# A decode layer on one core: the last weight matrix in two halves, its tail rows in one DMA, zero products between waits

## The chip, the cores and the metric

The kernel runs on one core of one Trainium2 chip. The metric is device time in microseconds (us), the median of several executions; the other cores are idle.

Names: PE is the matrix engine (TensorE), PEld its weight loads, DVE VectorE, ACT ScalarE, POOL GpSimd, SP SyncE, which issues most DMAs. SPq and ACTq are the DMA queues of SP and ACT.

## The reference, cut to what matters

```python
# A: attention over a cache, one query row per batch; B: a dense layer with mish
x = A_x                                           # (4, 1, 640)
h = x + A_ref(layernorm(x), k_cache, v_cache, wq, wo)   # caches (4, 32, 4096, 128) bf16
def B_ref(x, w1, b1, w2):                         # w1 (640, 1728), w2 (1728, 640)
    h = x @ w1 + b1
    act = h * tanh(softplus(h))
    return act @ w2
h2 = h + B_ref(layernorm(h), w1, b1, w2)
```

All arrays are bf16. The caches are 2 x 134 MB, nearly all of the traffic. The change concerns the short end: after the attention come wo, w1 and w2, 10 MB of weights, and the output of 4 x 640 numbers.

## The kernel before: the parts that matter

1728 = 13 x 128 + 64. So w2 has 13 full blocks of 128 rows (`FM` = 13) and a tail of 64 rows (`FT`). The full blocks are loaded in pieces: with runs of n rows, partition p holds n neighbouring rows of w2 in one contiguous packet of n x 1280 bytes (the trace has them: 5120 bytes for a run of 4 rows).

```python
    # SP: weights queue behind each other: wo, w1, the w2 tail, then w2 in 4 pieces
    w1_v = B_w1.rearrange("(p c) n -> p c n", c=DC)
    for k, (c0, c1) in enumerate(zip(W1S, W1S[1:])):          # three pieces
        load(sp, w1_sb[:, c0:c1, :], w1_v[:, c0:c1, :], ("w1", c0), f"W{len(WOS) + k}")
    for k in range(FT // 8):                                  # eight DMAs of 8 rows
        r = slice(k // 4 * 32 + k % 4, k // 4 * 32 + 32, 4)   # partitions 4 apart
        load(sp, w2_tail[r, :], B_w2[FM * P : F, :][r, :], ("w2t", k), "WT")
    ...
    for k, (j0, j1) in enumerate(zip(W2S, W2S[1:])):          # 4, 4, 4, 1 rows
        load(sp, w2_sb[:, j0:j1, :],
             B_w2[j0 * P : j1 * P, :].rearrange("(p j) n -> p j n", j=j1 - j0), ("w2", j0), ...)

    # PE: zero products whose result nobody reads; they keep PE busy
    def busy(n):
        for _ in range(n):
            mm(o_full[:, :], ident[:, :], zeros[:, 0:1].to_broadcast([P, 512]), True, True)
    ...
    busy(4)
    pe.need("act")
    def w2_mm(j):                     # one w2 row: four products of 160 columns
        rows = P if j < FM else FT    # on four column groups of PE, side by side
        for k in range(CG):
            cs = slice(k * OC, (k + 1) * OC)
            done = j == FM - 1 and k == CG - 1
            mm(y2_ps[k * QD : k * QD + N, :], act[0:rows, j, :],
               w2_sb[:, j, cs] if j < FM else w2_tail[0:FT, cs], False, j == FM - 1,
               "y2" if done else None)
    pe.need(("w2t", FT // 8 - 1))
    w2_mm(FM)
    for j0, j1 in zip(W2S, W2S[1:]):
        pe.need(("w2", j0))           # wait for this piece
        for j in range(j0, j1):
            w2_mm(j)

    # DVE casts all four quarters at once; SP and ACT issue two stores each
    dv.need("y2")
    dv.do(lambda: v.tensor_copy(out=o_bf[:, :], in_=y2_ps), "o_bf", DV)
```

Each list is the program of one engine, in its order; `need` is a wait on a semaphore. The engines work side by side in the timeline (at 653.03 us ACT, DVE and PE each start an operation), and so do the four products of a w2 row: a row takes 0.069 us at full clock though it streams 640 columns in all, where a zero product of 512 columns takes 0.22 us.

The softmax here doesn't subtract the row's maximum and nothing guards it: scores larger than these inputs give would overflow.

## Time and profile before

| | before |
|---|---|
| time, median of the first 3 runs | 661.67 us |
| span of the profiled run | 660.0 us |
| DMA engines busy | 90% or more in all slices but the last |
| act (input of w2's products) ready | 654.54 us |
| last two w2 pieces landed | 657.19 and 657.57 us |
| last product, last cast ended | 657.86, 658.23 us |

From the page of before, its first part and two lines on DMA. In the second line each digit is the busy share of a fortieth of the span in tenths, 9 meaning 90% or more.

```profile
span 660.0 us, 4989 instructions
...
PE 383.8 (58%) x2636; PEld 68.4 (10%) x1680; DVE 407.8 (62%) x257; ACT 40.7 (6%) x157; POOL 1.7 (0%) x12
...
DMA  9999999999999999999999999999999999999997
...
DMA packets 6954, 283.50 MB, mean 430 GB/s; under 512 B 857, under 2 KB 1184, under 8 KB 2208
```

The DMA engines are full until the last slice: the kernel is bound by moving 283.5 MB at 430 GB/s. The end is read from the timeline: start in us, length in us, engine, line, operation, number of instructions, and what ended the idle time before it.

```profile
653.49 1.49 PE L730 MATMUL o_ps<-zeros,ident 128*128 128x512 bf16 x3 [0.21 <-DMA w_tail<-in_B_w_dram]
...
655.13 1.27 PE L730 MATMUL red<-slotA,act 128*4 128x160 bf16 x32
...
657.23 0.62 PE L730 MATMUL red<-slotA,act 128*4 128x160 bf16 x20 [0.83 <-DMA slotA<-in_B_w_dram]
657.91 0.32 DVE L726 CAST o_bf<-red 128x160 bf16<-128x160 f32 x1 [3.37 <-PE red L730]
658.26 0.65 SPq L263 DMA_DIRECT2D out_dram<-o_bf  x2
```

PE runs through eight w2 rows, then waits for the last two pieces, and needs 0.62 us for their five rows; then come a cast and two stores on each queue. A wait of a group is printed only where it is long, and some records of products are missing: of the four zero products the first line has three. The windows view (length, then busy time and number of instructions of each engine, then the granted share of PE's clock, DMA share and GB/s) shows that PE ran at half its clock from about 653.4 to 656.8, without harm, since it waited for DMA afterwards:

```profile
650.00:652.00 2.00, 1.34 (x38) 1.21 (x35) 0.00 (x0) 0.47 (x1) 0.00 (x0) 1.00 1.05 407
652.00:654.00 2.00, 1.79 (x60) 1.43 (x59) 1.03 (x5) 0.25 (x1) 0.00 (x0) 0.84 1.00 410
654.00:656.00 2.00, 2.00 (x35) 0.81 (x37) 0.51 (x2) 0.00 (x0) 0.00 (x0) 0.50 0.86 345
```

The trace also has every DMA packet with its size and duration, and the time of each completion. A load of 128 rows leaves 16 of these reports; the eight 8-row DMAs of the tail left 72 (eight before 641.8 us, and 64 from 650.27 to 653.26). The trace does not name the DMA engine of a packet or of a report. "First", "mean" and "last" landing below are over the reports of one load.

### The profile page before, as it was taken

The page shows a single profiled execution, that of the slowest core. Times are in us where ns is not written, and L with a number is a line of the kernel's source. Part 1 is how long each engine was busy: PE and PEld are TensorE (multiplying, and loading weights), DVE is VectorE, ACT ScalarE, POOL GpSimd, SP SyncE. Part 2 cuts the span into 40 slices and gives each one's busy share as a digit, 9 for nine tenths or more (in the row PEclk, how much of TensorE's full clock was granted, in tenths as well). Part 3 has the DMA queues.
Part 4 walks back from the last instruction along what each step waited for, and adds up shares of the span by engine and source line. Part 5 has one row for each costly group of instructions (what it writes and reads, how often), then busy time and mean ns, then how long its engine had stood idle before and what let it go on. Part 6 is the DMA issues. An engine that isn't in the chain of part 4 may idle for free. (4 is left out here: it accounts for less than half of the span.)

```text
span 660.0 us, 4989 instructions
## 1 busy us (share of the span) xinstructions
PE 383.8 (58%) x2636; PEld 68.4 (10%) x1680; DVE 407.8 (62%) x257; ACT 40.7 (6%) x157; POOL 1.7 (0%) x12
## 2 busy tenths in 40 slices
PE   1255758457327595838307395838434757665877
PEld 0000100101101010101100010000110001010145
DVE  1087988386048778677219798749206688957612
ACT  0200000000000000000000000000000000000011
POOL 0000000000000000000000000000000000000000
PEclk9778787879659796869668887879876769796868
DMA  9999999999999999999999999999999999999997
GB/s 418 409 445 445 438 441 417 422 441 438 438 437 425 429 437 437 441 437 421 433 437 437 441 437 417 437 437 433 441 441 417 437 433 437 441 441 417 425 416 312
DMA packets 6954, 283.50 MB, mean 430 GB/s; under 512 B 857, under 2 KB 1184, under 8 KB 2208
## 3 DMA queue, kind: packets, MB, share of 16 engines
q1 hardware_dynamic: 6912, 283.35, 99.4%
q8 instruction: 7, 0.11, 0.1%
q14 instruction: 3, 0.02, 0.0%
q10 hardware_dynamic: 32, 0.01, 0.0%
HBM read 283.35 MB, written 0.01 MB: 429 GB/s over the span
## 5 line engine op out<-in xcount | busy, mean ns | idle before, releaser
L529 DVE TENSOR_TENSOR slotA<-slotA,q_bc 128x8192 bf16<-128x8192 bf16 x32 | 140.7, 4416 | 93.1 <-DMA slotA<-in_A_k_cache_dram 93.1
L529 DVE TENSOR_TENSOR slotB<-slotB,q_bc 128x8192 bf16<-128x8192 bf16 x32 | 140.7, 4418 | 18.4 <-DMA slotB<-in_A_k_cache_dram 18.4
L540 DVE TENSOR_REDUCE s_f<-red 128x64 f32<-128x1024 f32 x64 | 78.0, 1219 | 96.3 <-PE red L740 96.2
L740 PE MATMUL red<-slotA,ident 128*128 128x512 bf16 x480 | 135.8, 446 | 0.0
L740 PE MATMUL red<-slotB,ident 128*128 128x512 bf16 x480 | 126.1, 422 | 0.0
L730 PE MATMUL red<-slotA,ident 128*128 128x512 bf16 x32 | 14.7, 458 | 129.4 <-PEq L49 129.4
L730 PE MATMUL pv<-slotC,e 128*32 128x512 bf16 x768 | 51.9, 430 | 37.3 <-PEq L49 34.3
L730 PE MATMUL red<-slotB,ident 128*128 128x512 bf16 x32 | 14.2, 443 | 89.1 <-PEq L49 89.1
L406 ACT ACTIVATE ex<-s_f 128x64 bf16<-128x64 f32 x64 | 16.4, 256 | 513.3 <-DVE s_f L540 513.3
L554 DVE TENSOR_TENSOR e<-ex,hmask 128x512 bf16<-128x512 bf16 x64 | 39.8, 684 | 0.0
L730 PEld LDWEIGHTS pv<-slotC,e 128*32 128x32 bf16 x768 | 22.1, 106 | 95.4 <-issue 81.3
L730 PEld LDWEIGHTS red<-slotA,ident 128*128 128x128 bf16 x32 | 3.2, 99 | 198.0 <-issue 197.9
L730 PEld LDWEIGHTS red<-slotB,ident 128*128 128x128 bf16 x32 | 3.1, 98 | 171.1 <-issue 171.1
L730 PEld LDWEIGHTS o_ps<-pv_sb,selo 128*32 128x32 f32 x136 | 13.5, 109 | 62.6 <-issue 62.6
L730 PE MATMUL o_ps<-pv_sb,selo 128*32 128x128 f32 x136 | 18.0, 276 | 0.0
L730 PE MATMUL pv<-slotA,e 128*32 128x512 bf16 x256 | 14.5, 380 | 0.6 <-PEq L49 0.5
L416 ACT COPY pv_sb<-pv 128x512 f32<-128x512 f32 x16 | 9.4, 586 | 69.5 <-PE pv L730 69.5
L406 ACT ACTIVATION_READ_ACCUMULATOR ex<-s_f 128x1 f32 x64 | 11.9, 186 | 0.0
L730 PEld LDWEIGHTS pv<-slotA,e 128*32 128x32 bf16 x256 | 6.9, 97 | 23.6 <-issue 17.8
L579 DVE RECIPROCAL rl<-misc 32x1 f32<-32x1 f32 x4 | 0.6, 150 | 12.6 <-PE misc L730 12.6
L519 DVE CAST b1T<-pv 128x13 bf16<-128x13 f32 x1 | 0.2, 174 | 12.1 <-PE pv L730 12.1
L730 PE MATMUL y_ps<-a_t,slotB 128*128 128x64 bf16 x160 | 7.3, 211 | 0.0
(107 smaller groups left out, 69.2 us busy)
## 6 DMA issues: line engine op xcount, KB each, us to landing
slotC<-in_A_v_cache_dram SPq DMA_DIRECT2D x2, 4096.0 KB, 42.2
slotC<-in_A_wq_dram SPq DMA_DIRECT2D x1, 5120.0 KB, 15.4
slotB<-in_A_wo_dram SPq DMA_DIRECT2D x3, 1280.0 KB, 15.4
slotA<-in_B_w_dram SPq DMA_DIRECT2D x3, 640.0 KB, 13.9
slotB<-in_B_w_dram SPq DMA_DIRECT2D x2, 864.0 KB, 22.1
slotB<-in_A_wo_dram SPq DMA_DIRECT2D x1, 640.0 KB, 19.0
slotB<-in_A_wo_dram SPq DMA_DIRECT2D x1, 480.0 KB, 19.8
slotB<-in_B_w_dram SPq DMA_DIRECT2D x1, 432.0 KB, 22.8
```

What stands on the lines that cost most here:

```text
L406: lambda: a.activation(out=ex[:, sl], in_=s_f[:, sl], func=ACT.Exp, scale=SCALE, accum_out=rs[:, b, s : s + 1],),
L416: lambda: a.copy(out=pv_sb[:, :, :].rearrange("p r d -> p (r d)"), in_=pv[:, :]),
L519: dv.do(lambda: v.tensor_copy(out=b1T[:, 0:FM], in_=b1_ps[:, 0:FM]), "b1m", DV)
L529: lambda: v.tensor_tensor(out=t, in0=t, in1=q_bc[:, hg, b, :].unsqueeze(1).to_broadcast([P, RS, Dh]), op=ALU.mult,),
L540: lambda: v.tensor_reduce(out=s_f[:, s * RS : (s + 1) * RS], in_=red[:, k : k + 2, :].rearrange("p k (r c) -> p (k r) c", c=CW), axis=AX.X ...
L554: lambda: v.tensor_tensor(out=e[:, sl, :], in0=ex[:, sl].unsqueeze(2).to_broadcast([P, RS, G]), in1=hmask[:, :].unsqueeze(1).to_broadcast( ...
L579: dv.do(lambda: v.reciprocal(out=rl[:, :], in_=l_ps), ("rl", hg), DV)
L730: lambda: nc.tensor.matmul(out_, lhsT=lhsT, rhs=rhs, start=start, stop=stop, skip_group_check=skip),
L740: return t.add_instruction(mybir.InstMatmult(name=nc.get_next_instruction_name(), engine=mybir.EngineType.PE, ins=[t.lower_ap(rhs), t.lowe ...
```

## The change

Its intent: fewer, wider operations in the last stretch, and a PE that keeps its full clock. The output is made in two halves of 320 columns (each with its own cast, one on DVE and one on ACT, and its own store) instead of four quarters. w2 comes in runs of 5, 4, 3, 1 rows. All w1 pieces stream 64 columns instead of 64, 4, 4. Three zero products stand ahead of the third w2 piece. The tail rows come in one DMA. h is added by fp32 products instead of a bf16 high and low part, and b1 is loaded as one row.

```diff
-    FI = 4
+    FR = (5, 4, 3, 1)
-    OC = D // CG
+    KO = 2
+    OC = D // KO
@@ SP
-        for k in range(FT // 8):
-            r = slice(k // 4 * 32 + k % 4, k // 4 * 32 + 32, 4)
-            load(sp, w2_tail[r, :], B_w2[FM * P : F, :][r, :], ("w2t", k), "WT")
+        load(sp, w2_tail[0:FT, :], B_w2[FM * P : F, :], "w2t", "WT")
@@ PE, w1
-                    wd = WD if c0 == 0 else 1
                     mm(
-                        h1_w[0 : (P if j < FM else FT), j, 0:wd, :], w,
-                        cen[:, c, :].unsqueeze(1).to_broadcast([P, wd, N]), False, done,
+                        h1_w[0 : (P if j < FM else FT), j, :, :], w,
+                        cen[:, c, :].unsqueeze(1).to_broadcast([P, WD, N]), False, done,
@@ PE, h into the output: 40 bf16 products become 10 in fp32   (cut)
@@ PE, w2
-            for k in range(CG):
+            for k in range(KO):
                 ...
-                    y2_ps[k * QD : k * QD + N, :], act[0:rows, j, :],
+                    y2_ps[k * QD : k * QD + N, k, :], act[0:rows, j, :],
                     w2_sb[:, j, cs] if j < FM else w2_tail[0:FT, cs], False, j == FM - 1,
-        for j0, j1 in zip(W2S, W2S[1:]):
+        for j0, j1 in zip(FS, FS[1:]):
+            if j0 == FS[2]:
+                busy(3)
             pe.need(("w2", j0))
@@ ACT and DVE: one cast of 4 x 320 each; SP and ACT: one store each
+        ac.need(("y2", 1))
+        ac.do(lambda: a.copy(out=o_bf[QD : QD + N, :], in_=y2_ps[QD : QD + N, 1, :]), ("o_bf", 1), "AC")
-        dv.need("y2")
-        dv.do(lambda: v.tensor_copy(out=o_bf[:, :], in_=y2_ps), "o_bf", DV)
+        dv.need(("y2", 0))
+        dv.do(lambda: v.tensor_copy(out=o_bf[0:N, :], in_=y2_ps[0:N, 0, :]), ("o_bf", 0), DV)
@@ (cut: b1 as one row, zero products that load their weights once, unused tiles)
```

More of the change, by code (lines that the diff above doesn't have):

```diff
@@ L110 @@
     FC = FM + 1
-    FI = 4
-    FB = FM // FI
-    F0 = FB * FI * P
+    FR = (5, 4, 3, 1)
+    FS = [sum(FR[:k]) for k in range(len(FR) + 1)]
+    FG = [(k, i) for k, n in enumerate(FR) for i in range(n)]
+    assert FS[-1] == FM
     SLOT = R * Dh
@@ L125 @@
     WSEM = ["WQ", "WT"] + [f"W{k}" for k in range(13)]
-    for s in ["PE", "DV", "DVP", "DVA", "AC", "ACP", "PO", "KA", "KB", "VA", "VC", "V2", "X", "B0", "B1", "OUT0", "OUT1", "FIN"] + WSEM:
+    for s in ["PE", "DV", "DVP", "DVA", "AC", "ACP", "PO", "KA", "KB", "VA", "VC", "V2", "X", "B0", "OUT0", "OUT1", "FIN"] + WSEM:
         book.handles[s] = nc.alloc_semaphore(s)
@@ L176 @@
     wq = slot["C"][:, 0 : DC * H * Dh].rearrange("p (c n) -> p c n", c=DC)
-    b1r = sb("b1r", (FB, FI * P), BF16, setup, topC)
-    b1e = sb("b1e", (1, F - F0), BF16, setup, topC)
+    b1r = sb("b1r", (1, F), BF16, setup, topC)
     x_bf = sb("x_bf", (N, D), BF16, setup, topC)
@@ L196 @@
     ones_d = sb("ones_d", (P, P), FP32, tail, topA)
-    zeros = sb("zeros", (P, OC), BF16, tail, topA)
+    zeros = sb("zeros", (P, 1), BF16, tail, topA)
+    ident_f = sb("ident_f", (P, P), FP32, tail, topA)
     ysum = sb("ysum", (P, N), FP32, tail, topA)
@@ L210 @@
     b1_lo = sb("b1_lo", (P, FC, N), BF16, tail, topA)
-    h_hi = sb("h_hi", (P, DC, N), BF16, tail, topA)
-    h_lo = sb("h_lo", (P, DC, N), BF16, tail, topA)
     act = sb("act", (P, FC, N), BF16, tail, topA)
@@ L239 @@
     h1_ps = h1_w[:, 0:FC, 0, :]
-    y2_ps = red[:, 0, 0:OC]
+    y2_ps = red[:, 0:KO, 0:OC]
     x_rows = A_x.rearrange("b s d -> (b s) d")
@@ L246 @@
     W1S = (0, 2, DC - 1, DC)
-    W2S = tuple(range(0, FM, FI)) + (FM,)
     KS = {0: "A", 1: "B", 2: "A", 3: "B"}
@@ L255 @@
     dv = Prog(nc.vector, book)
-    pe = Prog(nc.tensor, book, take=["DVP", "DVA", "ACP", "VA", "VC", "V2"] + WSEM + ["B0", "B1"])
+    pe = Prog(nc.tensor, book, take=["DVP", "DVA", "ACP", "VA", "VC", "V2"] + WSEM + ["B0"])
     def tiles(src, i):
@@ L265, in store @@
     def store(p, h):
-        p.need("o_bf")
-        for k in range(h, CG, 2):
-            load(
-                p, out_rows[:, k * OC : (k + 1) * OC], o_bf[k * QD : k * QD + N, :],
-                ("out", k), f"OUT{h}",
-            )
+        p.need(("o_bf", h))
+        load(
+            p, out_rows[:, h * OC : (h + 1) * OC], o_bf[h * QD : h * QD + N, :],
+            ("out", h), f"OUT{h}",
+        )
     def leave(p, h):
@@ L276, in leave @@
             p.eng.sem_inc(fin, 1)
-            p.eng.wait_ge(o, 32).then_inc(o, -32)
+            p.eng.wait_ge(o, 16).then_inc(o, -16)
     def clear():
@@ L337, in sync_prog @@
             load(sp, w1_sb[:, c0:c1, :], w1_v[:, c0:c1, :], ("w1", c0), f"W{len(WOS) + k}")
-        for k in range(FT // 8):
-            r = slice(k // 4 * 32 + k % 4, k // 4 * 32 + 32, 4)
-            load(sp, w2_tail[r, :], B_w2[FM * P : F, :][r, :], ("w2t", k), "WT")
+        load(sp, w2_tail[0:FT, :], B_w2[FM * P : F, :], "w2t", "WT")
         sp.need(("PV", NT - 2))
-        for k, (j0, j1) in enumerate(zip(W2S, W2S[1:])):
+        for k, (j0, j1) in enumerate(zip(FS, FS[1:])):
             load(
@@ L368, in pool_prog @@
         po.do(lambda: g.memset(zeros[:, :], 0.0), "zeros", "PO")
+        po.do(lambda: g.tensor_copy(out=ident_f[:, :], in_=ident[:, :]), "ident_f", "PO")
     def act_prog():
         a = nc.scalar
-        load(ac, b1r[:, :], B_b1[0:F0].rearrange("(k f) -> k f", k=FB), "b1a", "B0")
-        load(ac, b1e[:, :], B_b1[F0:F].rearrange("(o f) -> o f", o=1), "b1b", "B1")
+        load(ac, b1r[:, :], B_b1.rearrange("(o f) -> o f", o=1), "b1", "B0")
         ac.need("eps", "mv")
@@ L441, in act_prog @@
             "ta", "AC",
+        )
+        ac.need(("y2", 1))
+        ac.do(
+            lambda: a.copy(out=o_bf[QD : QD + N, :], in_=y2_ps[QD : QD + N, 1, :]), ("o_bf", 1), "AC"
         )
@@ L664, in dve_prog @@
         )
-        dv.do(lambda: v.tensor_copy(out=h_hi[:, :, :], in_=st[:, :, :]), "h_hi", DV)
         dv.need("std2")
@@ L676, in dve_prog @@
         dv.do(lambda: v.reciprocal(out=rstd[:, :], in_=std2[:, :]), "rstd", DV)
-        dv.need("h_hi")
-        dv.do(
-            lambda: v.tensor_tensor(
-                out=h_lo[:, :, :], in0=st[:, :, :], in1=h_hi[:, :, :], op=ALU.subtract
-            ),
-            "h_lo", DV,
-        )
         dv.need("b1_hi")
@@ L734, in mm, with mm_same @@
         )
-    def mm_same(out_, lhsT, rhs, start, stop, mark=None):
+    def mm_same(out_, lhsT, rhs, start, stop, mark=None, skip=True):
         t = nc.tensor
@@ L746, in emit @@
                     tile_size=(P, P), tile_position=(0, 0), ldweights=False,
+                    bass_skip_group_check=skip,
                 )
@@ L750, in mm_same, with runs @@
         pe.do(emit, mark, "PE")
+    def runs(cols, j):
+        k, i = FG[j]
+        cols = cols[:, FS[k] * P : FS[k + 1] * P].rearrange("p (f i) -> p i f", i=FR[k])
+        return cols[:, i, :]
     def pe_setup():
@@ L784, in pe_setup @@
             )
-        pe.need("b1a", "b1b")
-        for k in range(FI):
-            mm(
-                b1_ps[:, k : FB * FI : FI], b1r[:, :].rearrange("k (f i) -> k i f", i=FI)[:, k, :],
-                ident[0:FB, 0:FB], True, True,
-            )
-        mm(b1_ps[:, FM - 1 : FM], b1e[:, 0:P], ident[0:1, 0:1], True, True)
-        mm(b1_ps[0:FT, FM:FC], b1e[:, P : P + FT], ident[0:1, 0:1], True, True, "b1p")
+        pe.need("b1")
+        for j in range(FM):
+            mm(b1_ps[:, j : j + 1], runs(b1r[:, :], j), ident[0:1, 0:1], True, True)
+        mm(b1_ps[0:FT, FM:FC], b1r[:, FM * P : F], ident[0:1, 0:1], True, True, "b1p")
     def fold(i, s):
@@ L808, in fold @@
                 )
-                mm(*args, skip=False) if first else mm_same(*args)
+                (mm if first else mm_same)(*args, skip=False)
     def pv_mm(i):
@@ L886, in busy @@
         def busy(n):
-            for _ in range(n):
-                mm(o_full[:, :], ident[:, :], zeros[:, 0:1].to_broadcast([P, 512]), True, True)
+            for k in range(n):
+                (mm_same if k else mm)(
+                    o_full[:, :], ident[:, :], zeros[:, :].to_broadcast([P, 512]), True, True
+                )
         hg = NHG - 1
@@ L897, in pe_tail @@
         pe.need("zeros", ("e", NT - 1, NS - 1))
-        for k in (2, 3):
-            mm(red[:, k, :], ident[:, :], zeros[:, 0:1].to_broadcast([P, 512]), True, False)
-        mm(y2_ps, ident[:, :], zeros[:, 0:OC], True, False)
+        for k, w in enumerate((OC, OC, 512, 512)):
+            (mm_same if k else mm)(
+                red[:, k, 0:w], ident[:, :], zeros[:, :].to_broadcast([P, w]), True, False
+            )
         wo_mm(2)
@@ L912, in pe_tail @@
                 pe.need("b1_lo")
-                for part in (b1_hi, b1_lo):
+                for n, part in enumerate((b1_hi, b1_lo)):
                     for j0, j1 in ((0, FC // 2 + 1), (FC // 2 + 1, FC)):
-                        mm(h1_ps[:, j0:j1, :], ident[:, :], part[:, j0:j1, :], False, False)
+                        (mm_same if n or j0 else mm)(
+                            h1_ps[:, j0:j1, :], ident[:, :], part[:, j0:j1, :], False, False
+                        )
             pe.need(("w1", c0))
@@ L918, in pe_tail @@
                 for c in range(c0, c1):
-                    if j < FB * FI:
-                        k, i = divmod(j, FI)
-                        w = w1_sb[:, c, k * FI * P : (k + 1) * FI * P]
-                        w = w.rearrange("p (f i) -> p i f", i=FI)[:, i, :]
-                    else:
-                        w = w1_sb[:, c, j * P : min((j + 1) * P, F)]
+                    w = runs(w1_sb[:, c, :], j) if j < FM else w1_sb[:, c, FM * P : F]
                     done = c == DC - 1 and j == FM - 1
-                    wd = WD if c0 == 0 else 1
                     mm(
-                        h1_w[0 : (P if j < FM else FT), j, 0:wd, :], w,
-                        cen[:, c, :].unsqueeze(1).to_broadcast([P, wd, N]), False, done,
+                        h1_w[0 : (P if j < FM else FT), j, :, :], w,
+                        cen[:, c, :].unsqueeze(1).to_broadcast([P, WD, N]), False, done,
                         "h1_ps" if done else None,
                     )
-        pe.need("h_lo", "h_hi")
-        for part in (h_hi, h_lo):
-            for k in range(CG):
-                for c in range(DC):
-                    mm(
-                        y2_ps[k * QD : k * QD + N, :].rearrange("b (m c) -> b c m", c=DC)[:, c, :],
-                        part[:, c, :], ident[:, k * QD : (k + 1) * QD], False, False,
-                    )
+        pe.need("st", "ident_f")
+        for c in range(DC):
+            for k in range(KO):
+                mm(
+                    y2_ps[k * QD : k * QD + N, k, :].rearrange("b (m c) -> b c m", c=DC)[:, c, :],
+                    st[:, c, :], ident_f[:, k * P // KO : (k + 1) * P // KO], False, False,
+                )
         busy(4)
@@ L944, in w2_mm @@
             rows = P if j < FM else FT
-            for k in range(CG):
+            for k in range(KO):
                 cs = slice(k * OC, (k + 1) * OC)
-                done = j == FM - 1 and k == CG - 1
                 mm(
-                    y2_ps[k * QD : k * QD + N, :], act[0:rows, j, :],
+                    y2_ps[k * QD : k * QD + N, k, :], act[0:rows, j, :],
                     w2_sb[:, j, cs] if j < FM else w2_tail[0:FT, cs], False, j == FM - 1,
-                    "y2" if done else None,
+                    ("y2", k) if j == FM - 1 else None,
                 )
-        pe.need(("w2t", FT // 8 - 1))
+        pe.need("w2t")
         w2_mm(FM)
-        for j0, j1 in zip(W2S, W2S[1:]):
+        for j0, j1 in zip(FS, FS[1:]):
+            if j0 == FS[2]:
+                busy(3)
             pe.need(("w2", j0))
```

## The prediction

> **What bounds the kernel now.** DMA does, almost to the end. In the page's slices the 16 DMA engines are 90% busy or more everywhere but the last slice, moving 283.5 MB at a mean 430 GB/s; PE is busy 58%, VectorE 62%. The chain of waits ends with the queue's issues, a 14.90 us wait for the w2 load, 0.65 us of PE and a 0.32 us cast. Weights are queued about 14 us before they land, so the queue does not run dry before 655 us. The change touches neither the attention loop nor the bytes of a load. Only what follows the last loads can move: 657.2 to 660.0 us.
>
> **The end before (trace, last 5 us).** w1's last piece lands at 651.9; act is ready at 654.54; the last two w2 pieces land at 657.19 and 657.57; the last product ends at 657.86, the cast at 658.23; two stores each are issued on SP and ACT from 658.26 (0.30 us each); the last store lands at 660.01.
>
> **What the change does there, costed.**
> 1. *w2 tail in one DMA.* The eight 8-row DMAs leave 64 engine completions plus eight immediate ones[...]. The completions of one load lie 1.8 us apart before the tail and 2.3 us after it[...]. A row of 1280 bytes takes 0.055 us. One 64-row DMA should give every engine 4 rows. I estimate the last landing 0.35 us earlier, 657.2.
> 2. *w2 in halves of 320.* A w2 row took 0.069 us at full clock with four 160-column products side by side (0.133 at half); two of 320 side by side should take twice that. But only one row now follows the last landing: +0.07 us.
> 3. *Cast of 320 columns in two engines.* VectorE: 0.32 + 160 columns at about 1 ns = 0.49 us; ScalarE about 0.45 (0.26 for 64 columns, 0.59 for 512). +0.17 us.
> 4. *One store per queue instead of two*: -0.35 us (second landing minus first, 659.64 to 660.01).
> 5. *fp32 identity products* in place of 40 bf16 ones: [...]behind act's wait. *w1 with 64 columns*: free, as 28 products took 1.22 us with 64 columns and 1.15 with 4. *Setup (b1 in one row)*: free; V's first load waits for it at 21.5 us while K loads fill the queue to 34 us.
>
> Sum: -0.35 + 0.07 + 0.17 - 0.35 = about -0.5 us.
>
> **The clock.** PE's granted clock was half from 653.37 to 656.79 and did not matter, as DMA came last. Now w2 needs 14 x 0.14 us warm, 14 x 0.27 cold, with 4 + 3 dummies of 0.21 or 0.43. Warm, PE waits for the last pieces. Cold, PE ends near 659 and the kernel loses about 1 us. The wider w1 products should keep it warm ([...]the trace's clock steps are 3.41 us apart). I give warm 70%.
>
> **Prediction: 661.2 us**, range 660.4 to 662.4; faster by over 2%: 0.01, within 2%: 0.98, slower: 0.01.
>
> **What would show it.** Last w2 landing near 657.2; completions of one load no wider than 2 us; last product near 657.6; casts 0.45 to 0.5 us; stores landed by 659.5; clock 1.0 after 653; loop slices unchanged.
>
> **What would make it wrong.** A cold clock; the two column halves not overlapping; engines whose raggedness does not come from the tail; a different state of the loop's DMA rate, worth more than all of this.

Four passages are cut out of the forecast, as marked, since no trace or run of this case shows them: in step 1 which DMA engines an 8-row DMA uses, and that the spreads agree with it; in step 5 a figure for the extra PE time; and a rule on what keeps the clock. -0.35 + 0.07 + 0.17 - 0.35 = -0.46, about -0.5 us. The first -0.35 is the author's estimate; what stands behind it are the two measured spreads (1.8 and 2.3 us) and the 0.055 us of a row, and its 4 rows an engine are 64 rows over the 16 DMA engines of the page. That the wider w1 products keep the clock was an estimate too, which experiment 3 tests. In the expectations below, passages are cut likewise.

## The result, and the profile after

| | median | lowest to highest | runs |
|---|---|---|---|
| before | 661.53 us | 661.38 to 661.82 | 6 |
| after | 661.58 us | 661.45 to 661.96 | 6 |

The ratio is 1.0001, 95% interval 0.9988 to 1.0014: the same time. A ratio here is the mean time of one kernel's fast runs over that of the other's of the same rounds, so not quite the ratio of the medians that are quoted. The time lies inside the predicted range of 660.4 to 662.4, but the predicted gain of 0.5 us is not there; a range 2 us wide that also holds the time of before is no evidence for the account.

The page of after:

```profile
span 660.1 us, 4898 instructions
...
PE 391.0 (59%) x2604; PEld 68.8 (10%) x1631; DVE 407.8 (62%) x255; ACT 41.1 (6%) x158; POOL 1.8 (0%) x13
...
DMA packets 6883, 283.48 MB, mean 429 GB/s; under 512 B 781, under 2 KB 1113, under 8 KB 2138
```

Its timeline for the end, the lines that answer to those of before:

```profile
654.06 0.82 PE L732 MATMUL o_ps<-zeros,ident 128*128 128x512 bf16 x3
...
655.33 1.46 PE L722 MATMUL red<-slotA,act 128*4 128x320 bf16 x18
...
656.94 0.60 PE L732 MATMUL o_ps<-zeros,ident 128*128 128x512 bf16 x2
...
657.47 0.71 PE L722 MATMUL red<-slotA,act 128*4 128x320 bf16 x8
658.21 0.48 DVE L718 CAST o_bf<-red 4x320 bf16<-4x320 f32 x1 [3.17 <-PE red L722]
658.25 0.42 ACT L441 CAST o_bf<-red 4x320 bf16<-4x320 f32 x1 [4.46 <-PE red L722]
...
658.72 0.35 SPq L262 DMA_DIRECT2D out_dram<-o_bf  x1
```

Its windows view, and the end of its chain of waits (start, length, what):

```profile
650.00:652.00 2.00, 1.12 (x30) 0.96 (x27) 0.00 (x0) 0.52 (x1) 0.00 (x0) 1.00 1.11 386
652.00:654.00 2.00, 2.00 (x53) 1.61 (x47) 0.59 (x3) 0.25 (x1) 0.00 (x0) 1.00 0.97 380
654.00:656.00 2.00, 1.78 (x16) 0.43 (x12) 0.94 (x4) 0.00 (x0) 0.00 (x0) 1.00 0.89 356
```

```profile
654.83 0.23 DVE act L711
...
655.10 1.68 PE red L722 x20
656.78 0.32 PE o_ps L722
657.10 0.43 PE o_ps L732 x2
657.54 0.69 PE red L722 x8
658.22 0.47 DVE o_bf L718
```

Two things differ from the forecast. First, the chain no longer ends at the last DMA: it comes from act through PE's rows, through the zero products (o_ps) and the last four rows. Second, the loads did not end earlier. From the trace's records:

```
                           before     after     difference   forecast
last w2 piece, last landing  657.57   657.57        0.00       -0.35
  from there to the end of the last product
                               0.29     0.61       +0.32       +0.07
cast (DVE)                     0.324    0.479      +0.16       +0.17
issue of the first store on SP to SP's last landing
                               1.75     1.37       -0.38       -0.35
```

The four differences add up to +0.10 us, which is the difference of the spans (660.0 and 660.1). So two of the four terms were right, and the two about the loads and PE were not. The experiments ask why.

### The profile page after: what moved, and what is told of

Its sections match the earlier page's. It is cut to its first block, busy times and chain, and to the rows that moved or that the text cites. A ratio compares the mean times of both kernels' runs of the same rounds, so it can differ in the third digit from the quotient of the medians.

```text
span 660.1 us, 4898 instructions
## 1 busy us (share of the span) xinstructions
PE 391.0 (59%) x2604; PEld 68.8 (10%) x1631; DVE 407.8 (62%) x255; ACT 41.1 (6%) x158; POOL 1.8 (0%) x13
## 5 line engine op out<-in xcount | busy, mean ns | idle before, releaser
L722 PE MATMUL red<-slotC,lnT 128*32 128x512 bf16 x40 | 4.5, 631 | 5.6 <-PEq L49 5.6
```

The costliest lines, as they stand in the source:

```text
L722: lambda: nc.tensor.matmul(out_, lhsT=lhsT, rhs=rhs, start=start, stop=stop, skip_group_check=skip),
```

## The experiments

Twelve kernels were run. Each was timed beside the kernel before on the same chip, or, where said, once. Every one passed the comparison with the reference, and this includes one whose result is wrong, so that comparison does not notice errors in the 64 tail rows.

### 1 and 2: no zero products at the third piece, and six

Theory: the zero products stand in PE's order ahead of rows that have landed already. Rival: the end hangs on the last landing, and the zero products cost nothing or hold the clock.

```diff
-            if j0 == FS[2]:
-                busy(3)            # experiment 1: none; experiment 2: busy(6)
```

> The kernel after without the three zero products ahead of the third w2 piece. Theory (they stand in the PE's order in front of rows that have already landed): the rows of the third piece start within 0.05 us of their landing (before this edit: landed 657.18, started 657.47), the last product ends 0.2 to 0.3 us earlier relative to the last landing, about 0.35 us after it instead of 0.61; the time falls by 0.25 us, which the rounds can hardly resolve. Rival (the end hangs on the last landing and on the wider cast alone, and the zero products are needed to keep the clock): no gain, or the clock falls to half and the last eight products take 0.27 us a row instead of 0.135, so it gets slower.

> The kernel after with six zero products instead of three at that place. Theory: the delay is paid one for one, three more at 0.22 us, so the last product ends 0.65 us later relative to the last landing (about 1.25 us after it) and the span is 0.65 us longer. Rival: slack swallows them, under 0.1 us.

Times: 661.54 us without (5 runs), 662.26 us with six (5 runs), 661.53 us for before (9 runs). The timeline without them, and then the chain of waits with six:

```profile
657.45 0.71 PE L722 MATMUL red<-slotA,act 128*4 128x320 bf16 x8 [0.44 <-DMA slotA<-in_B_w_dram]
...
658.19 0.48 DVE L718 CAST o_bf<-red 4x320 bf16<-4x320 f32 x1 [3.01 <-PE red L722]
```

```profile
655.02 1.76 PE red L722 x20
656.78 0.32 PE o_ps L722
657.10 1.09 PE o_ps L732 x5
658.19 0.68 PE red L722 x8
```

In experiment 1 the third piece landed at 657.40 and its rows started at 657.45; PE waited 0.44 us for it. The last piece landed at 657.79 and the last product ended at 658.16, 0.37 us later instead of 0.61. With six zero products it ended 1.29 us after the landing (657.54 to 658.83), and the median rose by 0.68 us over after. Both sizes fit the theory: three more zero products at 0.22 us each are paid in full, and without any PE waits for the third piece instead, so that 0.24 us are left to gain. The clock stayed at 1.0 without them. The 0.24 us of experiment 1 are not in its time, so this gain is shown in the trace alone. In that trace the first reports of all loads come 0.25 to 0.33 us later than in after from 188 us on, in the attention part, which the edit does not touch, and the last landing of w2 is 0.22 us later. So much can the long attention part vary from run to run; that it did so in all five runs is not shown.

### 3: w1 with 4 columns again

```diff
-                        h1_w[0 : (P if j < FM else FT), j, :, :], w,
-                        cen[:, c, :].unsqueeze(1).to_broadcast([P, WD, N]), ...
+                    wd = WD if c0 == 0 else 1
+                        h1_w[0 : (P if j < FM else FT), j, 0:wd, :], w,
+                        cen[:, c, :].unsqueeze(1).to_broadcast([P, wd, N]), ...
```

> The kernel after with w1's second and third pieces streaming 4 columns again. Theory of the clock: [...]the granted clock falls to half for 3.4 us as in the kernel before (0.50 from 654 to 656), the w2 rows take 0.27 us each and PE is 1 us or more late: span 660.8 to 661.5. Rival: zero products and w2 rows keep the clock at 1.0 anyway, span unchanged within 0.2 us.

Time: 662.98 us (662.44 to 663.89, 4 runs) against 661.53 us for before, ratio 1.0027, interval 1.0011 to 1.0042: slower, but far less than 2%. The windows view:

```profile
650.00:652.00 2.00, 1.15 (x32) 1.01 (x29) 0.00 (x0) 0.42 (x1) 0.00 (x0) 1.00 1.06 369
...
654.00:656.00 2.00, 2.00 (x10) 0.10 (x1) 0.84 (x3) 0.00 (x0) 0.00 (x0) 0.50 0.90 359
```

The clock fell to half from 652.70 to 656.12, so the zero products ahead of act took longer and w2's rows started at 656.0 instead of 655.1. The profiled span is 0.9 us over after's, the median 1.4 us. The theory holds: within the changed kernel the 64 columns are needed. Of the 14 kernels, the ten with 64 columns in all pieces of w1 kept 1.0 past the last product, and the four with 64, 4, 4 (before and experiments 3, 4 and 5) fell to half at 652.5 to 653.4. PE's busy share before the fall is the same either way: from 650 to 652 it is 1.15 us of 2.00 with 4 columns and 1.12 with 64, and in the last 3.41 us before the fall 2.51 us, against 2.54 us in after at that place. What differs is how many columns are streamed. The cold stretch lasted 3.42 us, as in before (3.41 us, 653.37 to 656.79). Why the clock falls was not shown.

### 4: the halves alone, on the kernel before

The edit takes over the two halves, two casts and two stores into before (four quarters out, the lines of the diff above); tail, runs, w1 and zero products stay as in before.

> The kernel before with the two 320-column halves alone (two casts, two stores, no other part). Theory by the terms: four rows after the third landing cost 0.14 us each instead of 0.07 (+0.25), the casts +0.15, one store per queue instead of two -0.37: span within 0.2 us of before. Rival (as predicted, halves are a gain of about 0.1 to 0.3 us since the rows hide behind the last landing): span 659.7 to 659.9.

Time: 661.42 us (4 runs) against 661.53 us for before; profiled span 660.1 us. The last piece landed at 657.70, the last product ended at 658.19, 0.49 us later, as the theory of the terms says (before 0.29). So 0.20 us on PE and 0.16 us on the casts use up the 0.38 us of the stores. The halves are worth nothing by themselves here. The rival's gain did not show.

### 5: the tail in one DMA alone, on the kernel before

```diff
-        for k in range(FT // 8):
-            r = slice(k // 4 * 32 + k % 4, k // 4 * 32 + 32, 4)
-            load(sp, w2_tail[r, :], B_w2[FM * P : F, :][r, :], ("w2t", k), "WT")
+        load(sp, w2_tail[0:FT, :], B_w2[FM * P : F, :], "w2t", "WT")
```

> The kernel before with the w2 tail rows in one DMA, nothing else. Theory A (the prediction's[...]): the completions of each w2 piece lie 1.8 us apart instead of 2.3, and the last w2 piece lands 0.3 to 0.4 us earlier, near 657.2. Rival B (one DMA itself holds w1's last piece and everything after it up, which would be why the kernel after gained nothing): w1's last piece lands near 652.3 instead of 651.9 and the last landing stays at 657.6. Rival C (the sum of the engines' work counts, not its spread): last landing unchanged, w1 unchanged.

Time: 661.43 us (4 runs) against 661.41 us for before (9 runs). The landings, from the trace's records; "slow" is the time by which all packets of cache and weight loads from 615 us on, taken together, exceeded the shortest time of a packet of their size:

```
                 w1's last piece   last w2 piece: first, mean, last     slow
before              651.91          655.24   656.36   657.57           2.4 us
experiment 5        652.33          655.95   656.77   657.60           9.3 us
after               652.36          655.79   656.68   657.57           7.6 us
```

Theory A was half right: the spread of the last piece shrank from 2.3 to 1.65 us. But its mean came 0.41 us later, and the two cancel in the last landing. Rival B holds: with nothing else changed, w1's last piece lands 0.42 us later, and packets are slow for two and a half microseconds from 650 on (5120-byte ones took 0.245 us in the mean, in before 0.204, at best 0.196). Rival C falls, as w1 moved. The sums fit: (9.3 - 2.4) us over 16 engines is 0.43 us each, and for after (7.6 - 2.4) / 16 = 0.33 against a mean that moved by 0.32. The windows view, the line of that stretch in before and in experiment 5; the last number is GB/s:

```profile
650.00:652.50 2.50, 1.84 (x49) 1.66 (x47) 0.00 (x0) 0.47 (x1) 0.00 (x0) 1.00 1.02 401
```

```profile
650.00:652.50 2.50, 1.36 (x34) 1.25 (x34) 0.00 (x0) 0.25 (x1) 0.00 (x0) 1.00 1.05 346
```

### 6 and 7: runs of 4, 4, 4, 1 and of 4, 5, 3, 1

Before experiment 5's result was known, the 6400-byte packets of the 5-row run looked guilty, since they are the ones that were slow in after. Both kernels differ from after in one line, `FR = (4, 4, 4, 1)` and `FR = (4, 5, 3, 1)`.

> The kernel after with w2 runs of 4, 4, 4, 1 rows as before. Theory D (the packets of the 5-row piece, 6400 bytes, took 0.27 to 0.30 us in the mean while it was read beside w1's end, against 0.244 for the fastest, and slowed w1's last packets; so the 5-row run costs about 0.35 us of DMA): with 5120-byte rows all packets take their 0.196 us, w1's last piece lands near 651.9 instead of 652.36, the last w2 piece near 657.2 instead of 657.57. Rival B (the one tail DMA does it, whatever the runs): w1 near 652.3, last landing 657.5. The end of PE is put off by the third piece's fourth row in either case.

> The kernel after with runs of 4, 5, 3, 1: the 5-row piece second. Theory D1 (rows of 6400 bytes are slow to read whenever they are read by all engines): its packets take 0.27 us or more in the mean again, now from 652 to 655, w1's last piece lands near 651.9 as it has no such neighbour, and the last landing stays near 657.5. Rival D2 (the time is slow, from 650 to 653, whatever is read then[...]): 5120-byte packets are slow there, and 6400-byte packets take 0.244.

Times: 661.58 us (4 runs), and 661.92 us in a single look, state unknown, against 661.41 us for before. Theory D fell. With rows of 5120 bytes these were slow in turn (0.240 us in the mean between 651 and 653, against 0.196 for the fastest), 8.0 us in all, and w1's last piece landed at 652.79. With the 5-row piece second, the 5120-byte packets of the first piece were slow between 651 and 653 (0.244), and the 6400-byte packets took 0.281 before 653 and 0.249 after it, nearly their best (0.244). So the slowness follows the place in the queue, right behind the tail, not the packet size.

### 8: runs of 4, 4, 3, 1, 1 without the zero products

> The kernel after with runs of 4, 4, 3, 1, 1 and without the three zero products. If theory D and the PE order hold: last landing near 657.2, last product 0.35 us after it at 657.55, stores landed near 659.45, so the span is 0.5 to 0.6 us under the kernel before (660.0) and the time near 661.0. If B holds: last landing 657.55, span 659.9.

Time: 661.44 us (5 runs) against 661.41 us for before; span 660.1 us. The last piece landed at 657.80 and the last product ended 0.34 us after it. PE's part came as expected, the landing did not, which again is rival B: the one-DMA tail was still there, and packets were slow by 8.8 us.

### 9: the changed kernel with the eight small DMAs

The edit of experiment 5, undone in after.

> The kernel after with the tail rows in eight DMAs again (undoes that part alone). Theory B (the one DMA slows the packets beside it; seen so far only by adding it to before): packets between 650 and 653 take their shortest time again (0.244 us for 6400 bytes instead of a mean near 0.29, excess over all packets about 2.4 us instead of 7.6), w1's last piece lands at 651.9, the mean completion of the last w2 piece comes 0.3 us earlier (656.35), but it is spread over 2.3 us again, so the last one stays near 657.6. Rival (another part of the change does it): packets stay slow.

The single time is 661.52 us, state unknown. Slow packets sum to 2.6 us, w1's last piece landed at 651.80, the last piece's mean is 656.37 and its last landing 657.59: as theory B expected, number by number. One DMA narrows the spread and slows the stream; eight DMAs leave the spread and slow the stream by much less. The time does not show it, since the end is the same. The zero products hold it here too: act was ready at 654.68, 0.36 us before after's 655.04, yet they began at 656.70 as in after (656.71), behind the rows of the second piece, which landed at 656.02 and 656.03. So in after this landing holds PE as much as act does: had act come earlier, the rows would have waited for the piece.

### 10: the tail DMA ahead of all weights, no zero products

```diff
+        load(sp, w2_tail[0:FT, :], B_w2[FM * P : F, :], "w2t", "WT")
         for n, (q, j0, j1) in enumerate(WOS):
             ...
-        load(sp, w2_tail[0:FT, :], B_w2[FM * P : F, :], "w2t", "WT")
```

> The kernel after without the three zero products and with the one tail DMA issued ahead of the first weight load, so nothing stands between w1 and w2. Theory B1 (the tail DMA itself slows its neighbours): packets at the change from w1 to w2 take their shortest time; slow ones appear near 624 to 633 if anywhere; if nothing is lost there the mean of the last piece is 656.35 with a spread of 1.8 us, so the last landing is 657.2, the last product 657.6, span 659.5 (-0.5), time about 661.0. Rival B2 (the engines go from w1 to w2 together and slow each other; the eight small DMAs only kept them apart): packets from 650 to 652.5 are slow again with no tail there, last landing 657.5, span 659.9.

Time: 661.35 us (661.11 to 661.58, 5 runs) against 661.63 us for before (9 runs). There are no slow packets at the change from w1 to w2 any more (1.0 us of slowness from 636 us on, none of it between 650 and 652.5). They are now where the tail is, which landed from 632.8 to 635.3: 7.1 us between 631.5 and 636, of which 5.9 us on wo's 10240-byte packets. The windows view of the same stretch in before and here:

```profile
632.00:634.50 2.50, 0.03 (x4) 0.06 (x8) 0.00 (x0) 0.00 (x0) 0.00 (x0) 0.50 0.90 382
```

```profile
632.00:634.50 2.50, 0.00 (x0) 0.00 (x0) 0.00 (x0) 0.00 (x0) 0.00 (x0) 0.50 0.93 328
...
650.00:652.50 2.50, 2.27 (x54) 2.06 (x54) 0.66 (x4) 1.49 (x2) 0.00 (x0) 1.00 1.04 429
```

Theory B1 holds, B2 falls: the tail's DMA itself slows what moves beside it, in both places where it stood (7.6 us in after, 7.1 us here). Moving it does not get the loss back: the last landing is 657.58. The span of 659.9 us is short by the stores' gain, since without zero products the last product ended 0.35 us after the landing.

### 11: the same DMA, other partitions (result wrong)

```diff
+        po.do(lambda: g.memset(w2_tail[:, :], 0.0), "w2tz", "PO")
-        load(sp, w2_tail[0:FT, :], B_w2[FM * P : F, :], "w2t", "WT")
+        sp.need("w2tz")
+        load(sp, w2_tail[0:P:2, :], B_w2[FM * P : F, :], "w2t", "WT")
```

> The kernel after with the 64 tail rows put on the even ones of 128 partitions (result wrong on purpose; the same reads from memory in the same place of the queue, only other partitions to write). Theory B3 (it is the write side[...]): packets take their shortest time, w1's last piece lands at 651.9, the last landing near 657.2. Rival B4 (read side, or the simple coming together of w1, tail and w2): slow packets as in the kernel after, excess 7 to 9 us, w1's last piece at 652.3.

One look; the single time is 661.30 us (state unknown), the span 659.8 us. Slow packets: 1.0 us. w1's last piece landed at 652.00, the last w2 piece at 655.29, 656.23 and 657.25 (first, mean, last). The stretch behind the tail in after and here:

```profile
650.00:652.50 2.50, 1.62 (x43) 1.35 (x36) 0.00 (x0) 0.52 (x1) 0.00 (x0) 1.00 1.06 366
```

```profile
650.00:652.50 2.50, 1.77 (x43) 1.46 (x37) 0.00 (x0) 0.44 (x1) 0.00 (x0) 1.00 1.03 425
```

Reading the same 80 KB in the same place of the queue, but writing them to the even ones of 128 partitions instead of to partitions 0 to 63, takes the whole loss away. So where the rows are written decides (B3 against B4): shown on this trace, and again in experiment 12. But the partitions alone do not decide it, as the eight DMAs of before and of experiment 9 write the same partitions 0 to 63 and slow the stream by 2.4 and 2.6 us only. Why the partitions matter was not shown: the trace names neither the DMA engine of a packet nor the place where it is written, and no other set of partitions was tried.

### 12: a version from the findings

The zero products at the third piece are taken out, and the tail rows go to even partitions with a right result. The activations of the tail are spread to even partitions by one product with an identity whose columns come twice, and one cast; the odd rows of the tail tile are zero. The tail's product moves behind the second piece, so that the cast is off the path.

```diff
+        po.do(lambda: g.memset(w2_tail[:, :], 0.0), "w2tz", "PO")
+        # twice[k, 2k] = twice[k, 2k + 1] = 1, from ident                (cut)
-        load(sp, w2_tail[0:FT, :], B_w2[FM * P : F, :], "w2t", "WT")
+        sp.need("w2tz")
+        load(sp, w2_tail[0:P:2, :], B_w2[FM * P : F, :], "w2t", "WT")
-        pe.need("w2t")
-        w2_mm(FM)
+        pe.need("twice")
+        mm(m_ps, twice[:, :], act[0:FT, FM, :], True, True, "at_ps")
         for j0, j1 in zip(FS, FS[1:]):
             if j0 == FS[2]:
-                busy(3)
+                pe.need("w2t", "act_t")
+                w2_mm(FM)              # act_t and 128 rows
@@ DVE
+        dv.need("at_ps")
+        dv.do(lambda: v.tensor_copy(out=act_t[:, :], in_=m_ps), "act_t", DVP)
```

> The kernel after without the three zero products, with the 64 tail rows on even partitions[...], and the tail's activations spread to the even partitions by one product and one cast, so that the result is right; the tail's product is moved behind the second w2 piece. Theory B3 plus the PE order: no slow packets (excess near 1.0 us), last landing 657.25 as in the run with wrong result, last product 0.35 us after it (0.60 with the zero products), last store 659.5, span 659.5 against 660.0 of before, time 661.0 (-0.5 against before of the same rounds, inside the interval of the rounds but visible in the medians). Rival: the spread product and its cast come on the path and the span is 659.8 or more.

Time: 660.78 us (660.74 to 660.90, 5 runs) against 661.48 us for before (661.34 to 661.57, 9 runs of the same rounds); ratio 0.9991, interval 0.9977 to 1.0004. The interval includes no difference; but all five runs lie below all nine, the lowest of which is 661.34. The timeline:

```profile
656.02 0.30 PE L735 MATMUL red<-w_tail,act_t 128*4 128x320 bf16 x2
...
656.65 0.71 PE L735 MATMUL red<-slotA,act 128*4 128x320 bf16 x8 [0.32 <-DMA slotA<-in_B_w_dram]
...
657.39 0.48 DVE L731 CAST o_bf<-red 4x320 bf16<-4x320 f32 x1 [2.37 <-PE red L735]
...
657.90 0.35 SPq L264 DMA_DIRECT2D out_dram<-o_bf  x1
```

Slow packets: 1.0 us. The last piece landed at 657.00 and the last product ended 0.36 us later; the span is 659.3 us, 0.7 us less than before. Of that, 0.57 us come from the last landing, about 0.25 us more than in experiment 11 could explain (657.25), which is the size of the run-to-run variation seen in experiment 1. The spread product and its cast stayed off the path: PE had them done when it waited for the third piece.

## Why the prediction was right or wrong

- **"DMA bounds the kernel; only what follows the last loads can move."** Right for the time, which differs by 0.05 us in 661. But the change also moved loads before that: w1's last piece landed 0.45 us later (652.36 instead of 651.91), and what failed in step 1 happened there, from 650 us on.
- **Step 1, "one 64-row DMA should give every engine 4 rows; last landing 0.35 us earlier".** This step failed. Its narrower spread was right and was seen: the completions of a piece lie 1.77 us apart instead of 2.33 (last minus mean 0.89 instead of 1.21). What was missing is a second effect of the same DMA, of the same size: it slows the packets beside it (7.6 us in all against 2.4), so the mean landing moved back by 0.32 us. The term measured 0.00 instead of -0.35. I had asked how the rows are shared among the engines that send, but not where they are written; experiment 11 shows that this matters as much.
- **Step 2, "+0.07 us on PE, only one row follows the last landing".** Wrong in size: +0.32. I counted the zero products at the third piece only as a risk to the clock, and in the text I even let PE wait for the last pieces in the warm case. In fact PE was still in them at 657.5 when the third piece landed at 657.18, and so four rows came behind the last landing instead of one. Without them the term is +0.08 (experiment 1, 0.37 against 0.29), which is the forecast.
- **Step 3, casts +0.17, and step 4, stores -0.35.** Right: +0.16 (160 more columns took DVE 0.155 us, 0.97 ns each) and -0.38.
- **Step 5, "free".** Right for the end as a whole: the fp32 products took 0.73 us (the 40 bf16 ones in before 0.61) and were over at 653.9, before act. The change of b1 moved nothing either: the first reports of the cache loads up to 623 us came within 0.1 us of those of before.
- **The clock, "70% warm".** Right: 1.0 from 639 to the end, and experiment 3 shows that it hangs on the 64 columns and what a cold clock would have cost, 0.9 us in the trace and 1.4 us in the median (forecast 1 us).

So the gain from the stores (0.38 us) was real and was used up by the zero products and the wider casts, and the gain from the tail was cancelled inside the DMA stream. That the last landing came out the same to 0.01 us is chance: two effects of one DMA happened to be of one size.

## What to carry to other kernels

When two pieces of a small load are merged into one, look where its partitions lie, not only at the number of packets: an 80 KB load to 64 neighbouring partitions cost a full stream 5 to 7 us of engine time, summed over 16 engines, and on the even ones of 128 partitions this loss was gone (1.0 us of slowness in all, against 7.6). How the load is cut counts too, as eight DMAs to the same 64 partitions cost far less (2.4 and 2.6 us of slowness in all, against 7.6 and 9.3 with one). A filler meant to keep PE warm stands in PE's order (three more zero products cost 0.68 us of the median), so put it where PE waits by more than the filler lasts, and see in the timeline whether real work had landed before it ended. And compare mean and spread of the completions apart: here both moved, by the same amount and against each other, and the last landing alone showed nothing.
